# Attention and a dense block on one core: all products as 64x32 weights in two row halves of TensorE

## The chip, the core and the metric

The kernel runs on one core of a Trainium2 chip. A core has TensorE (PE; its weight loads are shown apart as PEld), VectorE (DVE), ScalarE (ACT), GpSimd (POOL) and SyncE (SP), which work side by side and wait for each other on semaphores. Each engine runs its own list of instructions in order. Products land in PSUM, which has 8 banks of 128 partitions x 512 fp32 values; ScalarE and VectorE read them from there. The metric is the time of one execution in device microseconds; lower is better.

## What is computed

One layer on 2,048 rows of 640 values: a layer norm, and then the sum of the input, an attention block and a dense block, both on the normalised rows.

```python
B, S, D, H = 1, 2048, 640, 32;  Dh = D // H          # 20 values a head
q = (xn @ wq).reshape(B, S, H, Dh).transpose(0, 2, 1, 3)
k = xn @ wk                                          # one key and one value head
v = xn @ wv                                          # for all 32 query heads
p = softmax(einsum("bhqd,bkd->bhqk", q, k) * Dh ** -0.5)
o = einsum("bhqk,bkd->bhqd", p, v)
A = o.transpose(0, 2, 1, 3).reshape(B, S, H * Dh) @ wo
h = relu(xn @ w1 + b1) ** 2                          # 1,536 wide
out = x + A + (h @ w2 + b2)
```

## The kernel before

**Scores and exponentials.** The work is cut into 32 blocks (`NBLK`): 4 chunks of 512 queries by 8 groups of 4 heads. A block has 16 key tiles of 128 keys, and each key tile with a head is one score tile of 128 keys x 512 queries in one PSUM bank, 2,048 score tiles in all. A score tile is one matmul: the 20 rows of a head lie at partitions 32h to 32h+19 of `qT`, and of `kT`, which holds the keys four times, once for each head's place. So the weights are 20x128 at row position 32h (tile size 32x128), and up to four heads run at once in the four row groups, into different banks.

A score tile takes one of two ways. On the first, ScalarE does the exponential of two neighbouring banks (sometimes three or one) in one instruction (L1056) into `PT`. On the second, a *set* of one key tile and its four heads: VectorE writes the bits of a piecewise linear power of two from PSUM (L1245), GpSimd (L1265) or VectorE (L1267) makes three copies shifted by a constant, and a DMA with an add, issued by GpSimd (L1280), or VectorE may sum pairs of them. A set then enters the value product with up to four terms, the last two with scaled values `vxs`.

**Value products.** The values with a column of ones are the weights (`vx`, 128 keys x 32 columns, tile size 128x32), and the four heads go to the four column strips of one bank at once: four matmuls, one group. All products of a block add up in bank 7 (`PVB`), block after block; `emit_norm` copies the sum out (L1124), inverts the row of sums and brings both to the output layout by DMA.

**Dense work.** Queries, the first dense layer (L767, L775 behind it), the second dense layer with the output projection: all are `Unit`s, lists of chunks of four matmuls on the four column strips (`col4`, L561; `mm`, L426, is the line that all these matmuls have in the profile). One unit is open at a time, in a bank of its own. A 512-wide chunk is one fifth of a product over 640 rows; the 320-wide chunks are half a row of the output. The last row chunk's dense part is made early and parked in DRAM. The residual is loaded in 32 halves, and VectorE adds the bias to each (L823) before the output's evacuation adds it to the product (L854, L839).

**What sets the order.** No order is written out. While the program is built, a planner inside the kernel keeps a time for every engine, has a duration for every operation and takes, again and again, the operation that can start first, with priorities by kind. `make_step` picks the banks for ScalarE's next step, `make_dqk` opens a set, `make_pv` and `make_dpv` the value products, `pool_banks` says which banks may be taken by others. Its parameters change every 10 us of planned time (`RULES`). What comes out is one fixed list for each engine. TensorE's changes between the tile sizes 32x128 and 128x32 are charged in it (`SWITCH`), and matmuls that find no work ready may be filled with products of zeros (`fill_parts`).

Of the kernel before, what the change touches and what calls it, by code (L numbers as in the profile page):

```python
# [7 lines left out]
BF16 = mybir.dt.bfloat16  # L8
# [4 lines left out]
ALU = mybir.AluOpType  # L13
# [25 lines left out]
def _pl(z):  # L39
# [9 lines left out]
NB = 7  # L49
# [26 lines left out]
XSP = 1.0  # L76
# [6 lines left out]
SWITCH = 0.105  # L83
ACB, ACM = 0.0631, 0.4267
# [5 lines left out]
            fr=[f"OUT{16 + k // 2}.16" for k in range(8)])  # L90
# [8 lines left out]
RULES = {1: {'DGAP': 1.5, 'DLAST': 3.5, 'EPS': 0, 'M1T': 0.9, 'ADP': 0.35, 'R3': 2, 'D1P': 0.5, 'ND': 1, 'KEEP': 1, 'ADPM': 0.9, 'KEEPM': 3, 'DVL': 1.8},  # L99
         2: {'EVP': 1.1, 'DGAP': 0.5, 'IDLE': 0.3, 'EPS': 0.06, 'M1': 0, 'M1T': 0.9, 'ADP': 5, 'R3': 9, 'PP': 4, 'ND': 2, 'KEEP': 0, 'ADPM': 0.9, 'KEEPM': 3, 'PVA': 1},  # L100
         3: {'EVP': 1.1, 'DGAP': 0.5, 'IDLE': 0.3, 'EPS': 0.12, 'M1': 0, 'M1T': 2, 'ADP': 5, 'R3': 9, 'PP': 4, 'ND': 2, 'KEEP': 0, 'ADPM': 0.9, 'KEEPM': 3, 'JIT': 0.8},
         4: {'DGAP': 1.5, 'DLAST': 3.5, 'EPS': 0, 'M1T': 0.9, 'ADP': 0.9, 'R3': 2, 'D1P': 0.5, 'ND': 2, 'KEEP': 1, 'KEEPM': 1, 'DVL': 1.8, 'ADDB': 1, 'KEEPX': -1},
         5: {'DGAP': 1.5, 'DLAST': 3.5, 'EPS': 0, 'M1T': 0.9, 'ADP': 0.9, 'R3': 2, 'D1P': 0.5, 'ND': 2, 'KEEP': 1, 'ADPM': 0.9, 'KEEPM': 3, 'DVL': 1.8},
         6: {'DGAP': 1.5, 'DLAST': 3.5, 'EPS': 0, 'M1T': 0.9, 'ADP': 0.9, 'R3': 2, 'D1P': 0.5, 'ND': 2, 'KEEP': 1, 'ADPM': 0.9, 'KEEPM': 3, 'DVL': 1.8, 'SQP': 2},
         7: {'DGAP': 1.5, 'DLAST': 3.5, 'EPS': 0, 'M1T': 0.9, 'ADP': 0.9, 'R3': 2, 'D1P': 0.5, 'ND': 2, 'KEEP': 1, 'KEEPM': -1, 'DVL': 1.8, 'DQP': 0.5},
         8: {'DGAP': 1.5, 'DLAST': 3.5, 'EPS': 0, 'M1T': 0.9, 'ADP': 0.9, 'R3': 2, 'D1P': 0.5, 'ND': 2, 'KEEP': 1, 'DVL': 1.8, 'DQP': 0.5},
         9: {'DGAP': 1.5, 'DLAST': 3.5, 'EPS': 0, 'M1T': 0.9, 'ADP': 0.9, 'R3': 2, 'D1P': 0.5, 'ND': 2, 'KEEP': 1, 'ADPM': 0.9, 'KEEPM': 3, 'DVL': 1.8},
         11: {'DGAP': 1.5, 'DLAST': 3.5, 'EPS': 0, 'M1T': 0.9, 'ADP': 0.9, 'R3': 2, 'D1P': 0.5, 'ND': 2, 'KEEP': 1, 'KEEPM': 1, 'DVL': 1.8},
         12: {'DGAP': 1.5, 'DLAST': 3.5, 'EPS': 0, 'M1T': 0.9, 'ADP': 0.9, 'R3': 2, 'D1P': 0.5, 'ND': 2, 'KEEP': 1, 'KEEPM': 1, 'DVL': 1.8},
         13: {'ADP': 0.9, 'PBIAS': -1},  # L110
         14: {'DGAP': 1.5, 'DLAST': 3.5, 'EPS': 0, 'M1T': 0.9, 'ADP': 0.35, 'R3': 2, 'D1P': 0.5, 'ND': 2, 'KEEP': 1, 'KEEPM': 1, 'DVL': 1.8},
         15: {'DGAP': 1.5, 'DLAST': 3.5, 'EPS': 0, 'M1T': 0.9, 'ADP': 0.35, 'R3': 2, 'D1P': 0.5, 'ND': 2, 'KEEP': 1, 'KEEPM': 1, 'DVL': 1.8, 'ADPM': 3.5},
         16: {'EVP': 1.1, 'DGAP': 0.5, 'IDLE': 0.3, 'EPS': 0.06, 'M1': 0, 'M1T': 0.9, 'ADP': 5, 'R3': 9, 'PP': 4, 'ND': 2, 'KEEP': 0, 'ADPM': 0.9, 'KEEPM': 3},
         17: {'EVP': 1.1, 'DGAP': 0.5, 'IDLE': 0.3, 'EPS': 0.06, 'M1': 0, 'M1T': 0.9, 'ADP': 5, 'R3': 9, 'PP': 4, 'ND': 2, 'ADPM': 0.9, 'KEEPM': 3, 'KEEPX': 2},
         18: {'EVP': 1.1, 'DGAP': 0.5, 'IDLE': 0.15, 'EPS': 0.06, 'M1': 0, 'M1T': 0.9, 'ADP': 5, 'R3': 9, 'PP': 4, 'ND': 2, 'KEEPM': 3, 'KEEPX': 2, 'NOPEN': 3},
         19: {'EVP': 1.1, 'DGAP': 0.5, 'IDLE': 0.15, 'EPS': 0.06, 'M1': 0, 'M1T': 0.9, 'ADP': 5, 'R3': 9, 'PP': 4, 'ND': 2, 'KEEPM': 3, 'KEEPX': 2, 'NOPEN': 3},
         20: {'EVP': 1.1, 'DGAP': 0.5, 'IDLE': 0.15, 'EPS': 0.06, 'M1': 0, 'M1T': 0.9, 'ADP': 5, 'R3': 9, 'PP': 4, 'ND': 2, 'KEEPM': 3, 'KEEPX': 3, 'NOPEN': 3, 'BEHIND': 0.3},
         21: {'DGAP': 1.5, 'EPS': 0, 'M1T': 0.9, 'ADP': 0.9, 'R3': 2, 'D1P': 0.5, 'ND': 2, 'KEEP': 1, 'KEEPM': 0, 'DVL': 0.6},
         22: {'P2': 2, 'M1T': 2, 'KEEPM': 0, 'ADDM': 1.5},
         23: {'DLAST': 3.5, 'ADDB': 1},  # L120
         24: {'DGAP': 1.5, 'DLAST': 3.5, 'EPS': 0, 'M1T': 0.9, 'ADP': 0.9, 'R3': 2, 'D1P': 0.5, 'ND': 2, 'KEEP': 1, 'ADPM': 0.9, 'KEEPM': 3, 'DVL': 1.8},
         25: {'DGAP': 1.5, 'DLAST': 3.5, 'EPS': 0, 'M1T': 0.9, 'ADP': 0.9, 'D1P': 0.5, 'ND': 2, 'KEEP': 1, 'ADPM': 0.9, 'KEEPM': 3, 'DVL': 1.8},
         26: {'DGAP': 0},
         27: {'DGAP': 0, 'URG': 6, 'PVA': 1.05},
         28: {'DGAP': 1.5, 'DLAST': 3.5, 'EPS': 0, 'M1T': 0.9, 'ADP': 0.9, 'R3': 2, 'D1P': 0.5, 'ND': 2, 'KEEP': 1, 'ADPM': 0.9, 'KEEPM': 3, 'DVL': 1.8},
         29: {'DGAP': 0, 'DLAST': 3.5, 'EPS': 0, 'M1T': 0.9, 'ADP': 0.9, 'R3': 1, 'D1P': 0.5, 'ND': 2, 'KEEP': 1, 'ADPM': 0.9, 'KEEPM': 3, 'DVL': 1.8, 'KEEPX': -1},
         30: {'DGAP': 0, 'DRATE': 0.7, 'IDLE': 0.15, 'URG': 4, 'M1': 2, 'M1T': 2, 'ADP': 3.5, 'R3': 9, 'KEEPM': 0, 'KEEPX': 1, 'ADDM': 1.5},
         31: {'DGAP': 1.5, 'DLAST': 3.5, 'EPS': 0, 'M1T': 0.9, 'ADP': 0.9, 'R3': 2, 'D1P': 0.5, 'ND': 2, 'KEEP': 1, 'KEEPM': 1, 'DVL': 1.8, 'MRG': 0, 'MPRIO': 0.3},
         32: {'DGAP': 1.5, 'DLAST': 3.5, 'EPS': 0, 'M1T': 0.9, 'ADP': 0.9, 'R3': 2, 'D1P': 0.5, 'ND': 2, 'KEEP': 1, 'KEEPM': 1, 'DVL': 99, 'KEEPX': -1},
         33: {'DGAP': 1.5, 'DLAST': 3.5, 'EPS': 0, 'M1T': 0.9, 'ADP': 0.9, 'D1P': 0.5, 'ND': 2, 'KEEP': 1, 'KEEPM': 1, 'DVL': 1.8, 'P2': 1, 'PVD': 0.9},  # L130
         34: {'DGAP': 1.5, 'DLAST': 3.5, 'EPS': 0, 'M1T': 0.9, 'ADP': 0.9, 'R3': 2, 'D1P': 0.5, 'ND': 2, 'KEEP': 1, 'KEEPM': 1, 'DVL': 1.8},
         35: {'EVP': 1.1, 'DGAP': 0.5, 'IDLE': 0.3, 'EPS': 0.06, 'M1': 0, 'M1T': 0.9, 'ADP': 5, 'R3': 9, 'PP': 4, 'ND': 2, 'KEEP': 0, 'ADPM': 0.9, 'KEEPM': 3, 'P2': 1},
         36: {'EVP': 1.1, 'DGAP': 0.5, 'IDLE': 0.3, 'EPS': 0.06, 'M1': 0, 'M1T': 0.9, 'ADP': 5, 'R3': 9, 'PP': 4, 'ND': 2, 'KEEP': 0, 'ADPM': 0.9, 'KEEPM': 3},
         37: {'EVP': 1.1, 'DGAP': 0.5, 'IDLE': 0.3, 'EPS': 0.06, 'M1': 0, 'M1T': 0.9, 'ADP': 5, 'R3': 9, 'PP': 4, 'ND': 2, 'KEEP': 0, 'ADPM': 0.9, 'KEEPM': 3},
         38: {'EVP': 1.1, 'DGAP': 0.5, 'IDLE': 0.3, 'EPS': 0.06, 'M1': 0, 'M1T': 0.9, 'ADP': 5, 'R3': 9, 'PP': 4, 'ND': 2, 'KEEP': 0, 'ADPM': 3.5, 'KEEPM': 3},
         39: {'EVP': 1.1, 'DGAP': 0.5, 'IDLE': 0.3, 'EPS': 0.06, 'M1': 0, 'M1T': 0.9, 'ADP': 5, 'R3': 9, 'PP': 4, 'ND': 2, 'KEEP': 0, 'ADPM': 3.5, 'KEEPM': 3},
         41: {'DGAP': 1.5, 'DLAST': 3.5, 'EPS': 0.06, 'M1T': 0.9, 'ADP': 0.9, 'R3': 9, 'D1P': 0.5, 'ND': 2, 'KEEP': 1, 'KEEPM': 1, 'DVL': 1.8},
         42: {'DGAP': 1.5, 'DLAST': 3.5, 'EPS': 0.06, 'M1T': 0, 'ADP': 0.9, 'R3': 9, 'D1P': 0.5, 'ND': 2, 'KEEP': 1, 'KEEPM': 1, 'DVL': 1.8, 'BEHIND': 0.3},
         43: {'DGAP': 1.5, 'DLAST': 3.5, 'EPS': 0.06, 'M1T': 0, 'ADP': 0.9, 'R3': 9, 'D1P': 0.5, 'ND': 2, 'KEEP': 1, 'KEEPM': 1, 'DVL': 1.8, 'BEHIND': 0.3, 'URG': 6},
         44: {'EVP': 1.1, 'DGAP': 0.5, 'IDLE': 0.3, 'EPS': 0.06, 'M1': 0, 'M1T': 0.9, 'ADP': 5, 'R3': 9, 'PP': 4, 'ND': 2, 'KEEP': 0, 'ADPM': 0.9, 'KEEPM': 3},  # L140
         45: {'DGAP': 0, 'DRATE': 0.7, 'IDLE': 0.15, 'URG': 4, 'M1': 2, 'M1T': 2, 'ADP': 3.5, 'R3': 9, 'KEEPM': 0, 'KEEPX': 1, 'PP': 4, 'PVD': 1},
         46: {'EVP': 1.1, 'DGAP': 0.5, 'IDLE': 0.3, 'EPS': 0.06, 'M1': 0, 'M1T': 0.9, 'ADP': 5, 'PP': 4, 'ND': 2, 'KEEP': 0, 'ADPM': 0.9, 'KEEPM': 3, 'DQP': 0.5},
         47: {'DGAP': 1.5, 'DLAST': 3.5, 'EPS': 0, 'ADP': 0.9, 'R3': 2, 'D1P': 0.5, 'ND': 2, 'KEEP': 1, 'ADPM': 0.9, 'KEEPM': 3, 'DVL': 1.8, 'DQP': 0.5, 'P2': 2},
         48: {'EVP': 1.1, 'DGAP': 0.5, 'IDLE': 0.3, 'EPS': 0.06, 'M1': 0, 'M1T': 0.9, 'ADP': 5, 'R3': 9, 'PP': 4, 'ND': 2, 'KEEP': 0, 'ADPM': 0.9, 'KEEPM': 3},
         50: {'DGAP': 1.5, 'DLAST': 3.5, 'EPS': 0, 'M1T': 0.9, 'ADP': 0.9, 'R3': 2, 'D1P': 0.5, 'ND': 2, 'KEEP': 1, 'KEEPM': 1, 'DVL': 1.8, 'M1': 2},
# [88 lines left out]
class Op:  # L234
    def __init__(self, name, eng, dur, parts, deps=(), lat=None, lock=False, mode="C", prio=3, dma=None):
# [14 lines left out]
        if dma is not None:  # L250
            dma.n += 16
            self.tgt = (dma, dma.n)
# [1441 lines left out]
```

## Time and profile before

| | us |
|---|---|
| median of 3 runs | 676.48 |
| lowest, highest | 676.47, 681.13 |
| span of the profiled execution | 688.3 |
| busy in it: PE, ACT, DVE, POOL | 679.9, 657.7, 607.2, 586.2 |

The page of the profile gives each engine's busy time and, in 40 equal slices of the span, its share in tenths; a line of the same kind gives the clock that TensorE was granted. Other views group instructions by line and shape (busy time, mean length of one, idle time ahead of them), list who waited for whom, give busy time in chosen stretches, and list instructions in order of time. A matmul's length is modelled: about 0.39 us for 512 columns, though groups follow each other more closely, so that distances between starts tell more than lengths.

### The profile page before, as it was taken

The page shows a single profiled execution, that of the slowest core. Times are in us where ns is not written, and L with a number is a line of the kernel's source. Part 1 is how long each engine was busy: PE and PEld are TensorE (multiplying, and loading weights), DVE is VectorE, ACT ScalarE, POOL GpSimd, SP SyncE. Part 2 cuts the span into 40 slices and gives each one's busy share as a digit, 9 for nine tenths or more (in the row PEclk, how much of TensorE's full clock was granted, in tenths as well). Part 3 has the DMA queues.
Part 4 walks back from the last instruction along what each step waited for, and adds up shares of the span by engine and source line. Part 5 has one row for each costly group of instructions (what it writes and reads, how often), then busy time and mean ns, then how long its engine had stood idle before and what let it go on. Part 6 is the DMA issues. An engine that isn't in the chain of part 4 may idle for free.

```text
span 688.3 us, 22356 instructions
## 1 busy us (share of the span) xinstructions
PE 679.9 (99%) x9554; PEld 212.3 (31%) x9555; DVE 607.2 (88%) x1081; ACT 657.7 (96%) x721; POOL 586.2 (85%) x597
## 2 busy tenths in 40 slices
PE   8999999999999999999999999999999999999998
PEld 4233222232322222333332222333332222233334
DVE  8558999899999899889998999889888999999893
ACT  6668999999999999999999999999999999999994
POOL 0406989889999999989999989999989998989982
PEclk9559999999999999999999999999999999999999
DMA  8355677767877697768977667677777765788873
GB/s 215 89 130 145 130 158 149 152 138 156 168 166 143 124 176 136 155 133 179 200 140 154 134 131 136 135 150 147 141 160 152 141 124 115 152 180 185 169 158 97
DMA packets 62894, 102.21 MB, mean 148 GB/s; under 512 B 22418, under 2 KB 40722, under 8 KB 62794
## 3 DMA queue, kind: packets, MB, share of 16 engines
q0 software_dynamic: 19296, 70.26, 54.8%
q1 hardware_dynamic: 41898, 30.14, 16.6%
q8 instruction: 75, 1.23, 0.7%
q10 hardware_dynamic: 1600, 0.38, 0.3%
q14 instruction: 25, 0.20, 0.1%
HBM read 17.71 MB, written 4.42 MB: 32 GB/s over the span
## 4 chain that ended last, share of the span: by engine, by line
PE 74%; ACT 15%; POOL 5%; DVE 3%; DMA 2%; issue 1%; DVEq 0%; POOLq 0%
PE ps L426 71%; ACT PT L1056 15%; POOL x_sb L1265 2%; DVE tmore L1245 2%; POOL tmore L1265 2%; PE ps L619 1%; DMA x_sb<-x_sb 1%; DMA tmore<-tmore 1%; PE ps L648 1%; POOL x_sb L1280 1%; DVE big L775 0%; DVE xr L823 0%; DVE out_sb L1346 0%; PE ps L581 0%; PE ps L576 0%
## 5 line engine op out<-in xcount | busy, mean ns | idle before, releaser
L1056 ACT ACTIVATE PT<-ps 128x1024 bf16<-128x1024 f32 (+2 forms) x697 | 644.7, 1107 | 16.1 <-PE ps L426 15.5
L1245 DVE TENSOR_SCALAR tmore<-ps 128x512 uint16<-128x512 f32 x644 | 417.9, 682 | 43.9 <-PE ps L426 37.9
L1265 POOL INT64_ADD tmore<-tmore x226 | 258.8, 1306 | 35.9 <-DVE tmore L1245 25.9
L426 PE MATMUL ps<-qT,kT 20*128 20x512 bf16 x2048 | 277.1, 390 | 1.2 <-ACT PT L1056 0.8
L1265 POOL INT64_ADD x_sb<-tmore x222 | 255.8, 1287 | 21.4 <-PE ps L426 4.7
L426 PEld LDWEIGHTS ps<-qT,kT 20*128 20x128 bf16 x2048 | 68.8, 91 | 265.0 <-ACT PT L1056 218.4
L426 PE MATMUL ps<-PT,vx 128*32 128x512 bf16 x1396 | 139.5, 395 | 0.1
L426 PE MATMUL ps<-xnT,w_sb 128*32 128x512 bf16 x960 | 79.3, 383 | 0.4 <-DVE tmore L1245 0.4
L426 PE MATMUL ps<-w_sb,big 128*32 128x320 bf16 x1536 | 79.2, 301 | 0.3
L1280 POOL DMA_DIRECT2D tmore<-tmore x65 | 71.2, 1112 | 2.5 <-POOL tmore L1265 2.4
L1280 POOL DMA_DIRECT2D x_sb<-tmore x65 | 67.7, 1048 | 4.8 <-POOL x_sb L1265 3.3
L426 PE MATMUL ps<-tmore,vxs 128*32 128x512 bf16 x640 | 58.3, 382 | 0.3 <-POOL tmore L1265 0.3
L426 PE MATMUL ps<-x_sb,vxs 128*32 128x512 bf16 x624 | 57.6, 383 | 0.2 <-DMA x_sb<-x_sb 0.2
L426 PEld LDWEIGHTS ps<-PT,vx 128*32 128x32 bf16 x1396 | 35.2, 93 | 73.1 <-issue 67.5
L426 PE MATMUL ps<-tmore,vx 128*32 128x512 bf16 x456 | 43.3, 382 | 0.4 <-DMA tmore<-tmore 0.4
L426 PEld LDWEIGHTS ps<-w_sb,big 128*32 128x32 bf16 x1536 | 34.3, 96 | 28.4 <-issue 16.8
L767 DVE TENSOR_SCALAR hT_tmp<-ps,b1col 128x512 bf16<-128x512 f32 x48 | 35.5, 740 | 0.9 <-PE ps L426 0.6
L426 PE MATMUL ps<-xnT,wq_sb 128*32 128x512 bf16 (+2 forms) x480 | 35.8, 366 | 0.2 <-ACT PT L1056 0.2
L426 PE MATMUL ps<-wo_c,OC 128*32 128x320 bf16 x608 | 31.6, 301 | 0.0
L426 PE MATMUL ps<-x_sb,vx 128*32 128x512 bf16 x320 | 31.3, 382 | 0.0
L775 DVE TENSOR_TENSOR big<-hT_tmp 128x512 bf16<-128x512 bf16 x48 | 28.2, 589 | 0.2
L426 PEld LDWEIGHTS ps<-xnT,w_sb 128*32 128x32 bf16 x960 | 19.8, 95 | 22.0 <-issue 15.4
(103 smaller groups left out, 324.5 us busy)
## 6 DMA issues: line engine op xcount, KB each, us to landing
x_sb<-tmore POOLq DMA_DIRECT2D x65, 512.0 KB, 5.4
tmore<-tmore POOLq DMA_DIRECT2D x65, 512.0 KB, 5.6
w_sb<-in_B_w_dram SPq DMA_DIRECT2D x8, 480.0 KB, 4.3
big<-OR SPq DMA_DIRECT2D x71, 40.0 KB
big<-drs SPq DMA_DIRECT2D x71, 40.0 KB
xh<-in_A_x_dram SPq DMA_DIRECT2D x32, 80.0 KB, 3.4
out_dram<-out_sb SPq DMA_DIRECT2D x15, 160.0 KB, 2.8
qT<-QCr SPq DMA_DIRECT2D x105, 20.0 KB
```

The lines of the kernel that those rows point to most:

```text
L426: return lambda e: e.matmul(out_, l, r, start=start, stop=stop, tile_position=tp)
L619: return [lambda e: e.matmul(ps[:, PVB, :], ones_bf[:, :], hT_tmp[:, 0, :], start=True, stop=True)]
L648: return [(lambda e, dt=dt: e.transpose(out=psbf(bk)[:, dt * 128:(dt + 1) * 128], in_=xn_sb[:, st, dt * 128:(dt + 1) * 128], identity=iden ...
L767: o = Op(f"RL{qc}_{f}", "DVE", 0.66, [lambda e: e.tensor_scalar(out=hT_tmp[:, k % 2, :], in0=ps[:, bk, :], scalar1=b1col[:, f:f + 1], scal ...
L775: q = op(f"SQ{qc}_{f}", "DVE", 0.34, lambda e: e.tensor_tensor(out=h2T[:, f, :], in0=hT_tmp[:, k % 2, :], in1=hT_tmp[:, k % 2, :], op=ALU. ...
L1056: return Op(f"ACT{st_['j']}", "ACT", ACB + ACM * n, [lambda e: e.activation(out=to, in_=ps[:, b0:b0 + (n - 1) * db + 1:db, :], func=AF.Exp ...
L1245: d1 = op(f"D1_{n}_{i}", "DVE", 0.60, lambda e: e.tensor_scalar(out=L[:, cs].bitcast(U16), in0=ps[:, bank, :], scalar1=XA, scalar2=XB, op0 ...
L1265: fn = lambda e, T=T, j=j: e.int64_add(out=T.bitcast(I64), in0=L.bitcast(I64), in1=TSTEP * j * 0x0001000100010001)
L1280: p = op(f"AD{a}_{n}", "POOL", ADDUR, lambda e, src=src, dst=dst: e.dma_start(dst, src, accum_op=ALU.add), dp + [ad_last.get(k)], dma=adse ...
```

## The change

Behind the opening, every product has weights of 64 rows x 32 columns (tile size 64x32), so that the array is two row halves of four column strips. Each half is a *lane* with groups of four matmuls of its own.

- A 128-row product becomes two half groups, one in each lane, that add into the same bank. The lanes need not do their halves at the same time. A change of lane on a bank waits on a semaphore until the other lane's last group is done (`lane_ctr`; waits of TensorE for itself did not exist before).
- A score tile becomes one half group: the 64 rows hold two heads' places, and the four column strips take 32 keys each. `kT` is kept twice: copy 0 has the places of heads 0 and 2, copy 1 those of heads 1 and 3, the others multiplied by zero (`kmask`), so that one head of the pair is picked. Key and query weights are padded to 32 columns, and `qT` is set to zero once where no query is written. VectorE makes the second copy.
- All eight banks are in one pool; a block's sum may lie in any bank, and two blocks' sums may be open at once. ScalarE's step takes any two neighbouring banks, or three where many are free.
- Two (in one stage three) dense units may be open at once.
- The bias is no longer added to the residual by VectorE: an identity weight adds it on TensorE as the first chunk of each output half, and the evacuation takes the residual as loaded.
- The planner has a time for each lane, other constants, and new `RULES`. Merging of score groups of different kinds into one visit (`MRG`, `M1`, `P2`) is gone.

```diff
-NB = 7
+NB = 8
+SLOT, SLOT3, XLANE = 0.216, 0.136, 0.255
+HORD = (0, 2, 1, 3)
...
-        kT = sb("kT", [128, S], BF16)
+        kT = sb("kT", [128, 2, S], BF16)
...
         def start_of(op, r, switch=True):
+            if op.eng == "PE":
+                if op.lane is not None:
+                    s = max(r, pe_last[0], lanes[op.lane])
+                    if pe_mode[0] != "S":
+                        s = max(s, max(lanes) + (SWITCH if switch else 0.0))
+                    return s
...
+        def lane4(lane, lhs, rhs, bank, n, first, last):
+            w = slice(64 * lane, 64 * lane + 64)
+            return [mm(ps[32 * j:32 * j + 32, bank, 0:n], lhs(j)[w], rhs[w], first, last, (64 * lane, 32 * j)) for j in range(4)]
+
+        def key_parts(cs, src, k):
+            return lambda e: e.tensor_scalar(out=kT[:, k, cs], in0=src, scalar1=nk0[:, 1:2], scalar2=kmask[:, k:k + 1], op0=ALU.add, op1=ALU.mult)
...
+        def bias_chunk(cs):
+            return [(SLOT3, lambda lane, first, last: lane4(lane, lambda j: ident[:, 0:32], b2bc[:, cs], ub[0], 320, first, last))]
...
-            xs_op[n] = op(f"XS{n}", "DVE", 0.40, lambda e: e.tensor_tensor(out=xr[:, k % NXR, :], in0=xh[:, k % NXR, :], in1=b2bc[:, cs], op=ALU.add), [xr_op[n], l_b2, old], lock=True, prio=XSP)
...
-                parts.append(mm(ps[:, banks[k], :], kT[32 * h:32 * h + DH, kt * 128:(kt + 1) * 128], qT[32 * h:32 * h + DH, b % NQS, :], True, True, (32 * h, 0)))
-            qk = Op(f"QK{j}", "PE", 0.215, parts, deps, mode="R")
...
+        def qk_parts(b, kt, h, bank):
+            return lane4(h // 2, lambda j: kT[:, h % 2, kt * 128 + 32 * j:kt * 128 + 32 * j + 32], qT[:, b % NQS, :], bank, 512, True, True)
...
+        def pv_op(name, b, lane, wgt, srcs, deps, last, new_bank):
+            p = pvb.get(b)
+            if p is None:
+                deps.append(bank_rel[new_bank])
+            elif lane != p["lane"]:
+                deps.append(p["op"])
+            bank = new_bank if p is None else p["bank"]
+            w = slice(64 * lane, 64 * lane + 64)
+            parts = [mm(ps[32 * h:32 * h + 32, bank, :], wgt[w], srcs[h][w], p is None, last, (64 * lane, 32 * h)) for h in range(HPG)]
+            return Op(name, "PE", SLOT, parts, deps, lane=lane)
...
-                elif k == len(o.parts) - 1 and o.consumed:
-                    v = add(lists[o.eng], fn, waits=w, inc=eng_ctr[o.eng])
+                elif k == len(o.parts) - 1 and o.consumed:
+                    c = eng_ctr[o.eng] if o.lane is None else lane_ctr[o.lane]
+                    v = add(lists[o.eng], fn, waits=w, inc=c)
```

698 lines of the change are left out of this document (343 added, 355 removed), and 8 rows, old and new, of the table RULES.

## The prediction

> **What bounds the kernel now.** I read the page's busy shares and slices first, then ScalarE by stretches, then the groups, the waits and the raw order of TensorE in one short window.
>
> ```profile
> span 688.3 us, 22356 instructions
> PE 679.9 (99%) x9554; PEld 212.3 (31%) x9555; DVE 607.2 (88%) x1081; ACT 657.7 (96%) x721; POOL 586.2 (85%) x597
> ACT  6668999999999999999999999999999999999994
> PEclk9559999999999999999999999999999999999999
> 14.00:60.00 46.00, 44.94 (x471) 14.32 (x470) 28.01 (x81) 30.89 (x31) 11.65 (x14) 0.59 0.53 129
> 60.00:660.00 600.00, 597.39 (x8420) 180.04 (x8418) 551.84 (x921) 598.45 (x653) 559.79 (x565) 1.00 0.75 149
> 680.00:689.00 9.00, 4.93 (x140) 3.38 (x132) 5.56 (x12) 0.00 (x0) 0.00 (x0) 1.00 0.21 75
> ACT PT L1056 <- PE ps L426: 15.5, 23, 1.7
> ...
> 13.99 1.02 ACT L1056 ACTIVATE PT<-ps 128x1024 bf16<-128x1024 f32 x1 [0.81 <-PE ps L426]
> 268.08 14.81 ACT L1056 ACTIVATE PT<-ps 128x1024 bf16<-128x1024 f32 x16
> 674.72 4.68 ACT L1056 ACTIVATE PT<-ps 128x1536 bf16<-128x1536 f32 x4
> ```
>
> The rows by stretches give busy time and count of PE, PEld, DVE, ACT, POOL, then the clock. From 60 to 660 us ScalarE is busy for 598.45 of 600 us and TensorE for 597.39: both are full at once. ScalarE's waits for TensorE are 15.5 us in all, and the 14 to 60 us stretch, where it is busy for only 30.89 of 46, holds nearly all of them. There the granted clock is 0.59 on average and 0.5 in two slices; after that it is 1.00. The last three rows (start, length) are ScalarE's first exponentials, an undisturbed run of 16, and the last ones, which end at 679.4.
>
> **The base of the sum.** The profiled execution spans 688.3 us, the median of the runs is 676.48: 11.8 us less. I put this on the half clock, since the stretch that has it is the only one in which ScalarE starves (15.1 of its 46 us) and 11.8 fits inside. So the sum is made on the span and 11.8 us is taken off: a timed run is 14.0 us before the first exponential, ScalarE's stretch of 679.4 - 14.0 - 11.8 = 653.6, and 688.3 - 679.4 = 8.9 us behind it: 676.5.
>
> **Part 1: ScalarE's work.** The order of the built programs has 671 exponentials of two tiles, 14 of three and 12 of one before (and 4 of two into other buffers), 1,404 tiles; after, 696 of two, one of three and one of one, 1,396 tiles.
>
> ```profile
> L1056 ACT ACTIVATE PT<-ps 128x1024 bf16<-128x1024 f32 x671 | 623.4, 1107 | 14.3 <-PE ps L426 13.8
> L1056 ACT ACTIVATE PT<-ps 128x1536 bf16<-128x1536 f32 x14 | 20.3, 1502 | 1.7 <-PE ps L426 1.7
> L1056 ACT ACTIVATE PT<-ps 128x512 bf16<-128x512 f32 x12 | 8.0, 663 | 0.0
> ```
>
> A tile more costs (1502 - 663)/2 = 420 ns. Eight tiles fewer are 8 x 0.42 = **-3.4 us**, on the path, as ScalarE is full. "Any neighbouring banks" does not make steps larger: the triples go from 14 to 1. This work bounds the gain. The undisturbed run takes (14.81 - 1.107)/15 = 0.914 us a step of two; by it the work before is 675 x 0.914 + 14 x 1.334 + 12 x 0.494 = 642 us of the 653.6, and after 696 x 0.914 + 1.334 + 0.494 = 638. So before loses 12 us in all to waits and short delays, and no better feeding can bring more than that.
>
> **Part 2: TensorE's work.** The rows of one window (start, length, matmuls) give the price of a score group between the other products.
>
> ```profile
> 299.71 0.39 PE L426 MATMUL ps<-qT,kT 20*128 20x512 bf16 x4
> 300.03 0.40 PE L426 MATMUL ps<-PT,vx 128*32 128x512 bf16 x4
> 300.26 0.72 PE L426 MATMUL ps<-w_sb,big 128*32 128x320 bf16 x16
> 300.91 0.39 PE L426 MATMUL ps<-qT,kT 20*128 20x512 bf16 x2
> 301.23 0.32 PE L426 MATMUL ps<-w_sb,big 128*32 128x320 bf16 x4
> ...
> 664.44 0.39 PE L426 MATMUL ps<-x_sb,vx 128*32 128x512 bf16 x4
> 664.65 0.39 PE L426 MATMUL ps<-x_sb,vxs 128*32 128x512 bf16 x4
> ```
>
> Groups of four 512-wide products start 664.65 - 664.44 = 0.21 us apart (I take 0.215; 300.26 - 300.03 gives 0.23). Four 320-wide groups last 0.72 against 0.32 for one: (0.72 - 0.32)/3 = 0.135 each. A score group holds the engine 301.23 - 300.91 = 0.32 us, so 0.32 - 0.215 = 0.10 is the change of tile size; ahead of it the same again, 300.91 - 300.26 - 4 x 0.135 = 0.11. The order has 685 visits to score groups, 1,215 groups of 512 and 552 of 320: 685 x 0.42 + 1215 x 0.215 + 552 x 0.135 = 288 + 261 + 75 = 624 us.
>
> After, the 1,379 changes of tile size fall to 29. A 2,048-tile score pass becomes 2,048 half-array groups of four. In all the order has 4,516 half groups of 512, 1,136 of 320 (the bias rows that replace the VectorE add among them: 32 of these, 32 x 0.135/2 = 2 us) and 60 of 256 at about 0.11: (4516 x 0.215 + 1136 x 0.135 + 60 x 0.11)/2 = 565 us with both halves always full. They are not: TensorE runs its list in order, and in 1,065 places a group follows one on its own half, so the other half stays empty behind it. Walking the order with these durations, a group starting neither before the one ahead of it nor before its half is free, gives 618 us.
>
> New too are 616 waits of TensorE for itself: products of both halves add into one bank, so a change of half on a bank waits until the other half's last product has landed. 356 of the 616 stand at a value product of ScalarE's tiles. Behind each stand, in the same list, the next score groups, for which ScalarE waits. The trace of before has no such wait. The nearest row is ScalarE waiting for a score group:
>
> ```profile
> 303.85 0.39 PE L426 MATMUL ps<-qT,kT 20*128 20x512 bf16 x2
> 304.28 1.02 ACT L1056 ACTIVATE PT<-ps 128x1024 bf16<-128x1024 f32 x1 [0.19 <-PE ps L426]
> ```
>
> From start to the waiter's start are 304.28 - 303.85 = 0.43 us. Walking the order again with 0.43 from the awaited group's start gives 632 us; with no wait beyond the slot 621; with the 0.10 of a tile-size change on top (0.53) 654. I take 632, the row that also ends in a semaphore wait for a product. Most are covered: 429 of the 616 have two or more groups of the waiter's own half between. So TensorE needs 621 to 654, likely 632, against 624: **+8 us of work (-3 to +30), no relief**. It has that room: the window from its first score group to its end is about 660 us without the slow clock. I price it at 0 to +2 us of time, with 0 taken as long as the need stays under some 645 us; beyond that every microsecond counts.
>
> [...] Before has 9,554 matmuls, the new order 23,167. In the trace the four matmuls of a group start within 10 ns (0.40 us for x4, where one lasts 395 ns by its group's row below). [...]
>
> **Part 3: VectorE, GpSimd, banks.**
>
> ```profile
> L426 PE MATMUL ps<-PT,vx 128*32 128x512 bf16 x1396 | 139.5, 395 | 0.1
> L1245 DVE TENSOR_SCALAR tmore<-ps 128x512 uint16<-128x512 f32 x644 | 417.9, 682 | 43.9 <-PE ps L426 37.9
> L823 DVE TENSOR_TENSOR xr<-xh,b2bc 128x320 f32<-128x320 bf16 x32 | 22.2, 696 | 0.0
> L1267 DVE TENSOR_SCALAR x_sb<-tmore 128x2048 uint16<-128x2048 uint16 x18 | 14.0, 775 | 0.1
> L663 DVE TENSOR_SCALAR kT<-ps,nk 128x256 bf16<-128x256 f32 x6 | 2.9, 484 | 11.0 <-PE ps L426 10.9
> L1265 POOL INT64_ADD tmore<-tmore x226 | 258.8, 1306 | 35.9 <-DVE tmore L1245 25.9
> L1280 POOL DMA_DIRECT2D tmore<-tmore x65 | 71.2, 1112 | 2.5 <-POOL tmore L1265 2.4
> ```
>
> VectorE loses 32 bias adds (-22.2). It gains 18 shifted copies (53 against 35, 18 x 0.775 = +14.0), 8 score tiles (8 x 0.682 = +5.5) and the second key copy (6 x 0.484 + 4 x 0.35, its row in part 4, = +4.3): +1.6 in all, and it is idle for 48 us between 60 and 660. GpSimd loses 12 copies and 12 sum DMAs, 12 x 1.306 + 12 x 1.112 = -29. SP issues the same 596 instructions. All this is cover, not path: 0. Eight banks in one pool with the value sums wandering among them (450 of 1,756 half groups in bank 7, the rest in others) free no engine that is late.
>
> **Part 4: opening and end.** The second key copy stands ahead of the first scores.
>
> ```profile
> 12.06 1.12 ACT L602 ACTIVATE qT<-ps 128x128 bf16<-128x128 f32 x4 [0.34 <-PE ps L426]
> 12.30 0.35 DVE L600 TENSOR_SCALAR kT<-ps,nk 128x128 bf16<-128x128 f32 x1
> ```
>
> The query copies on ScalarE end at 12.06 + 1.12 = 13.18; two key copies of 0.35 us from 12.30 end at 13.0. So the copies hide the second one: 0, or +0.35 if they were gone. At the end the sum of the last block and the last output halves each need a change of half, 0.43 - 0.215 = 0.2 each: +0.4.
>
> Sum: 676.5 - 3.4 + 0.4 + (0 to 2) = 673.5 to 675.5, less what falls of the 12 us that ScalarE loses, now that any two neighbouring banks serve it and a score group needs no change of tile size: between 0 and 12, and I take 3, a quarter, as TensorE is as full as before. That is **671 us**, -0.8%.
>
> **The rivals.** One per cent (6.8 us) is what a measurement of this kernel tells from no change.
>
> - *The plan hides every change of half.* TensorE needs 621 us, ScalarE runs at its undisturbed rate: 14.0 + 638 + 8.9 = 661 us. For it: 429 of 616 are well covered. Against it: it means that all 12 us go, the opening's too.
> - *The changes of half cost more (the other side).* Place: the value products, 356 of the waits, with scores queued behind. Price: 0.53 us from the awaited start, a need of 654, 22 more than taken: 671 + 22 = 693 us. It decides from a need of about 645. For it: the list is strict, and the need climbs by 22 us for 0.10 us of wait.
> - *The clock stays at a half in the opening of the timed runs:* 671 + 11.8 = 683 us. The profiled run of before had it, two of three timed runs seem not to. [...]
> - *Matmul starts have a floor.* The widest bound from rows is 0.135/4 = 34 ns per matmul, as 320-wide strips never went faster: 22,848 x 0.034 = 777 us, so 671 + 777 - 632 = 816 us.
> - *The change doesn't do what it says:* the halves don't run beside each other. Then 2 x 565 = 1,130 us of slots, and some 1,160 us. Before shows four column strips at once and up to four row groups at once, never both.
>
> **How the numbers follow.** Chances: forecast 0.45 (its own range 666 to 678), hidden 0.22, dearer changes 0.17, slow clock 0.08, start floor 0.05, halves in turn 0.03. Faster by over 1% (under 669.7): 0.22 and three tenths of the forecast, 0.36. Slower (over 683.2): 0.17 + 0.04 + 0.05 + 0.03 = 0.29. Within: 0.35. The range 660 to 692 leaves out the last two, a third of the dearer case and a tail of the fastest: under 0.2.
>
> **What would show it.** Part 1: 698 exponentials of about 1.1 us, and ScalarE busy for 598 of 600 us again. Part 2: half groups of both halves 0.21 us apart on each half, no 0.10 at scores, waits of TensorE for itself that end 0.43 us behind the awaited start. If ScalarE idles on TensorE between 60 and 660 us, I am wrong by Part 2; if the eight starts of a pair spread over 0.2 us, the floor holds. Half clock outside the opening would be wrong for all cases.

## The result and the profile after

The changed kernel takes **815.86 us** (median of its runs) against 676.48: ratio 1.205, 95% interval 1.197 to 1.212. It is slower by a fifth; the forecast was 671, its range ended at 692. The profiled execution has a span of 813.7 us. One of the three executions fell into a slower state (830.04 us), and runs that were made only once (experiments 2, 3, 5, 6 and 8 to 10) can't be told apart in this way, so that steps of some 2% between them mean little.

The page of the profile after: span, busy time by engine, ScalarE's busy tenths, the granted clock, the queue that brings instructions, and the chain that ended last.

```profile
span 813.7 us, 50344 instructions
...
PE 724.5 (89%) x23167; PEld 413.6 (51%) x23167; DVE 611.4 (75%) x1089; ACT 669.3 (82%) x718; POOL 560.6 (69%) x574
...
ACT  7859889877888787788798988897999989997760
...
PEclk9979999999999899999999999999999999999999
...
q8 instruction: 181, 2.97, 1.5%
...
PE 83%; issue 10%; POOL 3%; DVE 3%; DMA 1%; ACT 0%; DVEq 0%; POOLq 0%
```

ScalarE no longer stands at 9 in every slice, and no slice shows half clock. "Issue" is 10% of the chain: time in which an engine waited for nothing that the profile shows. The window between opening and end, with the columns of the prediction's window (busy time and count of PE, PEld, DVE, ACT, POOL, then clock, DMA share and GB/s):

```profile
60.00:780.00 720.00, 642.07 (x20921) 365.28 (x20913) 555.67 (x921) 620.09 (x657) 539.39 (x546) 0.98 0.60 120
```

The list of waits of the same run (us in total, times, longest):

```profile
PEld ps L443 <- issue: 126.9, 161, 3.4
...
ACT PT L1105 <- PE ps L443: 113.0, 105, 3.6
PE ps L443 <- issue: 76.5, 73, 3.1
...
PEld ps L443 <- PE ps L443: 33.2, 104, 1.1
```

Everyone now waits for TensorE: ScalarE is busy for 620 of 720 us, where it was 598 of 600. TensorE waits for "issue" first; its waits for itself, the changes of half, come far behind. Of the two rows of "issue", that of the matmuls (PE) is the one to go by. The weight loads had even more of it in the kernel before, but in short waits that the matmuls covered; the matmuls themselves waited 0.9 us for it there, in two places.

```profile
PEld ps L426 <- issue: 175.6, 705, 0.8
```

One such place in order of time (start, length, and in brackets the idle time ahead with what ended it):

```profile
295.63 3.98 ACT L1105 ACTIVATE PT<-ps 128x1024 bf16<-128x1024 f32 x4
302.84 2.89 ACT L1105 ACTIVATE PT<-ps 128x1024 bf16<-128x1024 f32 x3 [3.23 <-PE ps L443]
...
302.28 0.61 PE L443 MATMUL ps<-qT,kT 64*32 64x512 bf16 x11 [3.13 <-issue]
```

TensorE stands still for 3.13 us with nothing to wait for, and ScalarE for 3.23 us right behind it.

Split by ScalarE's exponentials: in the kernel before, 14.0 us lie ahead of the first, 653.6 us (half clock taken off) between first and last, 8.9 behind. After, it is 14.8, 774.4 and 24.5: +0.8, +120.8 and +15.6. Of the 120.8, ScalarE's idle time between exponentials is 109 (114.0 against 16.7 less the 11.8 of half clock). Most of the other 12 goes with the pauses too: exponentials in a row start 0.905 us apart (the median in the kernel before), though one behind a pause lasts 1.02. A pause so loses an overlap of 0.115 us, and 82 pauses more (105 against 23) lose 9.4. The base of the prediction is a little off here: a run's time is 1.8 us more than its span (815.51 against 813.7), so that not 11.8 but 13.6 us had to come off the span before. With that the three parts add up to the 139 us between the two times.

**Where TensorE stands still.** An instruction packet on queue 8 is 16,384 bytes and there is one for every 256 of TensorE's matmuls and weight loads: 46,334/181 after. The kernel before had this row, which I had not read:

```profile
q8 instruction: 75, 1.23, 0.7%
```

It had 19,109 of them: 255 a packet. I took all gaps of over 0.35 us between starts on TensorE and set them beside the packets' transfers. After has 164 such gaps, 145.0 us in all; 104 of them, 117.0 us, end 1.1 to 1.75 us behind the end of a packet's transfer, and their places in the list step by 255.6 instructions a packet. Before, 4 gaps (2.2 us) do, no more than chance would put there: the 0.65 us behind each of 75 packets are 7% of the span, and it has 94 gaps. After, chance alone would give some 24 of the 164, but 93 of the 104 (112 us) also lie within 12 instructions of one even grid. From the start of a packet's transfer to the first instruction behind such a gap it is 2.1 to 3.3 us, median 2.42.

### The profile page after: what moved, and what is told of

The parts are those of the page before. It is cut to its first block, busy times and chain, and to the rows that moved or that the text cites. A ratio compares the mean times of both kernels' runs of the same rounds, so it can differ in the third digit from the quotient of the medians.

```text
span 813.7 us, 50344 instructions
## 1 busy us (share of the span) xinstructions
PE 724.5 (89%) x23167; PEld 413.6 (51%) x23167; DVE 611.4 (75%) x1089; ACT 669.3 (82%) x718; POOL 560.6 (69%) x574
## 4 chain that ended last, share of the span: by engine, by line
PE 83%; issue 10%; POOL 3%; DVE 3%; DMA 1%; ACT 0%; DVEq 0%; POOLq 0%
PE ps L443 82%; DVE tmore L1359 1%; POOL tmore L1379 1%; PE ps L649 1%; POOL x_sb L1379 1%; DMA xnT<-big 1%; POOL tmore L1394 0%; POOL x_sb L1394 0%; DVE OR L1224 0%; PE ps L705 0%; ACT PT L1105 0%; PE ps L609 0%; PE ps L604 0%; PE ps L737 0%; DVE big L517 0%
## 5 line engine op out<-in xcount | busy, mean ns | idle before, releaser
L1105 ACT ACTIVATE PT<-ps 128x1024 bf16<-128x1024 f32 (+1 forms) x694 | 656.6, 1034 | 114.8 <-PE ps L443 113.0
L443 PE MATMUL ps<-qT,kT 64*32 64x512 bf16 x8192 | 510.0, 385 | 27.6 <-issue 25.7
L1359 DVE TENSOR_SCALAR tmore<-ps 128x512 uint16<-128x512 f32 x652 | 423.0, 685 | 118.5 <-PE ps L443 114.8
L443 PE MATMUL ps<-PT,vx 64*32 64x512 bf16 x2776 | 273.8, 385 | 7.5 <-issue 5.4
L443 PEld LDWEIGHTS ps<-qT,kT 64*32 64x32 bf16 x8192 | 163.0, 91 | 150.5 <-issue 42.8
L443 PE MATMUL ps<-w_sb,big 64*32 64x320 bf16 x3072 | 150.7, 303 | 16.3 <-issue 16.2
L443 PE MATMUL ps<-xnT,w_sb 64*32 64x512 bf16 x1920 | 141.0, 382 | 6.0 <-issue 6.0
L443 PE MATMUL ps<-x_sb,vxs 64*32 64x512 bf16 x1296 | 124.1, 385 | 5.4 <-issue 5.0
L443 PE MATMUL ps<-tmore,vxs 64*32 64x512 bf16 x1272 | 119.0, 381 | 6.6 <-issue 5.0
L443 PE MATMUL ps<-tmore,vx 64*32 64x512 bf16 x1016 | 100.1, 383 | 0.3 <-POOL tmore L1379 0.2
L443 PEld LDWEIGHTS ps<-w_sb,big 64*32 64x32 bf16 x3072 | 78.7, 94 | 38.3 <-issue 22.1
```

The source lines that it names most:

```text
L443: return lambda e: e.matmul(out_, l, r, start=start, stop=stop, tile_position=tp)
L1105: return Op(f"ACT{st_['j']}", "ACT", ACB + ACM * n, [lambda e: e.activation(out=to, in_=ps[:, b0:b0 + (n - 1) * db + 1:db, :], func=AF.Exp ...
L1359: d1 = op(f"D1_{n}_{i}", "DVE", 0.60, lambda e: e.tensor_scalar(out=L[:, cs].bitcast(U16), in0=ps[:, bank, :], scalar1=XA, scalar2=XB, op0 ...
```

## The experiments

Three theories, by the letters that the expectations use. **D**: TensorE's list is delivered in packets of 256 instructions, too slowly for 23,167 matmuls with a weight load each. **H**: the waits between the row halves cost more than the 0.43 us that the prediction took. **M**: each matmul start has a price of its own (34 ns, the prediction's fourth rival). One table for all runs of a whole kernel; "gaps" are those at packets, counted as above, and the idle time is that of ScalarE ahead of its pairs of score tiles.

| run | matmuls + loads | packets | gaps, us | ScalarE idle, us | time, us |
|---|---|---|---|---|---|
| kernel before | 19,109 | 75 | 4, 2.2 | 14.3 | 676.5 |
| kernel after | 46,334 | 181 | 104, 117.0 | 114.8 | 815.9 |
| one strip | 22,598 | 88 | 2, 1.1 | 22.7 | 702.0 |
| one strip, more loads | 34,466 | 135 | 28, 26.2 | 32.8 | 716.4 |
| one strip in scores | 34,046 | 133 | 34, 37.7 | 39.5 | 727.8 |
| one strip in dense work | 36,638 | 143 | 32, 29.9 | 40.1 | 725.1 |
| plan spaced by 0.108 us | 46,006 | 180 | 81, 102.8 | 120.6 | 833.1 |
| plan spaced by 0.145 us | 45,326 | 177 | 66, 38.0 | 55.6 | 898.3 |
| kernel before, more loads | 26,157 | 102 | 4, 2.1 | 4.5 | 683.6 |
| fewer, larger matmuls | 23,402 | 92 | 1, 0.5 | 414.3 | 1,167.4 |

**1. The same plan with fewer instructions.**

```diff
-return [mm(ps[32 * j:32 * j + 32, bank, 0:n], lhs(j)[w], rhs[w], first, last, (64 * lane, 32 * j)) for j in range(4)]
+return [mm(ps[32 * j:32 * j + 32, bank, 0:n], lhs(j)[w], rhs[w], first, last, (64 * lane, 32 * j)) for j in range(STRIPS)]
```

`STRIPS` is 1. In experiments 1 to 4 the first warm-up products of the opening also go to all eight banks instead of one.

> The changed kernel with the same planned order, the same waits, the same banks and the same exponentials, but every half group of a score tile, of a dense step and of an output product sends only the first of its four 64x32 matmuls (columns 0 to 31); the value products keep all four. Three quarters of the scores and of the dense sums are so not computed. TensorE's list falls from 23,167 matmuls to 11,299, the instruction packets from 181 to about 90. Theory D (delivery of instructions: TensorE gets its list in packets of 256 instructions, and a packet takes 2.1 to 3.3 us from its start to the first instruction out of it, some 3.5 us from packet to packet, so that more than 256 instructions in 3.5 us run dry): the starts no longer wait at packets, ScalarE's exponentials stand beside one another again, and the time falls to 665 to 690 us, about where the recorded sum put it. Theory H (the waits between the two row halves cost more than 0.43 us): all 616 waits are still there, the time stays over 780. Theory M (a start price for each matmul, 34 ns): 11,299 times 34 ns is 384 us, so it would fall as well, but no gap would stand at the packets in the changed kernel's trace, where 104 do.

Measured: 702.0 us, ratio 1.036 (1.033 to 1.040). Its page and waits:

```profile
q8 instruction: 88, 1.44, 0.8%
...
L1110 ACT ACTIVATE PT<-ps 128x1024 bf16<-128x1024 f32 (+1 forms) x694 | 642.8, 1063 | 22.7 <-PE ps L444 21.6
```

```profile
PEld ps L444 <- PE ps L444: 28.9, 96, 0.6
...
ACT PT L1110 <- PE ps L444: 21.6, 24, 6.0
...
PEld ps L444 <- issue: 10.5, 43, 0.6
```

Of the 139 us between the two times, 114 are gone, and with them the waits for "issue": the loads' row falls from 126.9 us to 10.5, none longer than 0.6, and the matmuls' row of 76.5 us is empty. Three quarters of the products of scores and dense work are gone as well; experiment 4 takes that up. TensorE's waits for itself are nearly all still there (28.9 against 33.2), so theory H, which asked for over 780, falls as the main cause. But the expectation was missed too: 702 lies 12 us above its upper end. Even with its list at hand this plan is 25 us behind the kernel before. By the same split: +0.5 ahead of the first exponential, +14.8 in the stretch, +9.8 behind the last (18.7 us). In the stretch ScalarE idles 21.8 us, 7.0 of them from 20 to 60 us and 8.1 behind 660. Pieces of the chain there (start, length, what):

```profile
651.77 6.67 DMA drs<-R
...
660.57 7.06 DMA big<-drs
...
668.79 29.65 PE ps L444 x328
```

The last sums' way through DRAM and back, and behind it 29.65 us of TensorE with outputs and the last products, set the end.

**2 and 3. One strip in the scores alone, and in the dense work alone.** The scores in `qk_parts`, then the dense layer's and the output's calls of `lane4`.

```diff
-    return lane4(h // 2, lambda j: kT[:, h % 2, kt * 128 + 32 * j:kt * 128 + 32 * j + 32], qT[:, b % NQS, :], bank, 512, True, True)
+    return lane4(h // 2, lambda j: kT[:, h % 2, kt * 128 + 32 * j:kt * 128 + 32 * j + 32], qT[:, b % NQS, :], bank, 512, True, True)[:1]
```

> The changed kernel with only the first of the four 64x32 matmuls of each half group of the scores; dense steps, output and value products whole. Three quarters of the scores are not computed. 17,023 matmuls, about 134 instruction packets in place of 181. Theory D: at 3.5 us from packet to packet the floor is 134 times 3.5 = 469 us in place of 634 us, with bursts in the dense steps still running dry: 690 to 740 us, and the gaps at packets fall from 104 to 30 to 60. Theory H: over 780 us.

> The changed kernel with only the first of the four 64x32 matmuls of each half group of the dense layer (both weights) and of the output products; scores, queries, keys and values whole. Three quarters of those dense sums are not computed. 18,319 matmuls, about 144 instruction packets in place of 181, but the stretches with scores and value products stay as thick with instructions as in the changed kernel. Theory D, between the two runs on record (17,023 matmuls: 727.8 us, 11,299: 702.0) and the changed kernel (23,167: 815.9): 725 to 760 us, gaps at packets between 30 and 80. Theory H: over 780.

Measured: 727.8 and 725.1 us, both as theory D had it, the second at the very edge of its range. The count of gaps (34 and 32) is at the low end of what was expected. Whichever part of the list is thinned, about as many instructions give about the same time.

**4. The instructions without the work.** Experiments 1 to 3 leave out products as well as instructions. Here instructions that do nothing are put back.

```diff
+PADS = 3
...
+def padded(e):
+    for _ in range(PADS):
+        e.ldweights(zeros32[w], tile_position=(64 * lane, 0))
+    return e.matmul(ps[0:32, bank, 0:n], lhs(0)[w], rhs[w], start=first, stop=last, tile_position=(64 * lane, 0))
+return [padded]
```

> The run with the first of four matmuls only (702.0 us, ratio 1.036), same matmuls, plan, waits and banks, and ahead of each matmul that stands for a half group three weight loads of zeros that nothing uses: 11,868 more instructions and no more products. Three quarters of the scores and of the dense sums are not computed. About 134 instruction packets in place of 88, as many as the run with the scores cut (133; 727.8 us). Four loads of 23 ns each (three extra loads a matmul took 92 ns a matmul when measured alone) fit under a half group of 215 ns. Theory D, the count of instructions alone: gaps at packets come back, 20 to 60, and the time goes up to 715 to 740 us. If instead the matmuls left out were what the shorter runs saved: 700 to 706 us, no gaps.

Measured: 716.4 us, ratio 1.060 (1.055 to 1.064), against 1.036 (1.033 to 1.040) without the loads.

```profile
q8 instruction: 135, 2.21, 1.2%
...
L1114 ACT ACTIVATE PT<-ps 128x1024 bf16<-128x1024 f32 (+1 forms) x694 | 649.2, 1034 | 32.8 <-PE ps L592 26.5
```

The gaps at packets come back, 28 with 26.2 us, and the time rises by 14 us, though no product was added. It is less than the 26 us of experiment 2 at the same count. The loads stand in other places, and that run was taken once only; what makes the difference was not tried.

**5. The delivery by itself.**

```diff
+def both(form, n, count):
+    for g in range(count):
+        form(0, (2 * g) % 8, n)
+        form(1, (2 * g + 1) % 8, n)
+    mark()
...
+both(half, 512, 200)
+both(half, 320, 200)
+both(half, 128, 200)
```

`half` is four 64x32 matmuls in one row half, as in `lane4`; `mark` is twelve full-array products that set the stretches apart.

> TensorE alone, on zeros; nothing of the reference is computed and the output is zeros. One after the other: 200 times both row halves (eight 64x32 matmuls) at 512 columns, at 320, at 128; 200 groups of one half at 512; 200 pairs of 64x128 matmuls at 512 and 320 and 400 pairs at 128; then 60 half groups of 512 columns that change halves each time behind a semaphore. Theory D, at 3.5 us for a packet of 256 instructions or 27 ns for a matmul with its weight load: 27 to 28 ns a matmul with both halves at 512 (the work alone asks 26.9), 27 at 320 (the work: 16.7) and 27 at 128 (the work: 6.7), with gaps every 256 instructions; 54 ns with one half alone; the 64x128 pairs are bound by work at 512 and 320 (0.215 and 0.136 us a pair). Theory M, a start price of 34 ns: 34 ns a matmul in all three stretches with both halves, evenly spread. Theory H: a half that waits for the other starts more than 0.5 us behind it; the recorded sum had 0.43.

Measured, per matmul from the first start of a stretch to the last: 28.0 ns at 512 columns, 26.8 at 320, 27.3 at 128; one half alone at 512 53.8; pairs of 64x128 at 512 0.215 us. The stretch at 320 columns in order of time, then that at 128:

```profile
65.02 3.86 PE L308 MATMUL ps<-mv,wt 64*32 64x320 bf16 x215
69.87 2.37 PE L308 MATMUL ps<-mv,wt 64*32 64x320 bf16 x128 [0.99 <-issue]
73.33 2.37 PE L308 MATMUL ps<-mv,wt 64*32 64x320 bf16 x128 [1.09 <-issue]
77.05 2.37 PE L308 MATMUL ps<-mv,wt 64*32 64x320 bf16 x128 [1.36 <-issue]
...
117.24 1.91 PE L308 MATMUL ps<-mv,wt 64*32 64x128 bf16 x128 [2.46 <-issue]
120.97 1.91 PE L308 MATMUL ps<-mv,wt 64*32 64x128 bf16 x128 [1.82 <-issue]
124.70 1.91 PE L308 MATMUL ps<-mv,wt 64*32 64x128 bf16 x128 [1.82 <-issue]
```

This is theory D by itself: exactly 128 matmuls, which with their loads are 256 instructions, then a hole, and 3.45 to 4.01 us from one such run to the next, however short the matmuls are. The windows of the three stretches (length, PE busy, PEld busy, ..., clock):

```profile
17.20:62.10 44.90, 44.44 (x1601) 25.10 (x1600) 0.00 (x0) 0.00 (x0) 1.00 0.02 4
65.00:108.00 43.00, 29.49 (x1601) 25.11 (x1600) 0.00 (x0) 0.00 (x0) 1.00 0.02 5
110.70:154.50 43.80, 22.55 (x1601) 20.01 (x1600) 0.00 (x0) 0.00 (x0) 0.56 0.02 4
```

Three stretches with 1,600 matmuls take 43 to 45 us each, though PE is busy for 44, 29 and 23 of them; even half clock (0.56) in the third changes nothing. The DMA share is 0.02, so the delivery is slow without any other traffic. From the start of a packet's transfer to the first matmul behind a hole it is 2.48 us (median), as in the changed kernel (2.42). Between the holes the matmuls start 16.4 ns apart on average at 320 columns and 11.8 at 128, and the first eight of each stretch, four in each half, start within 24 ns: theory M's 34 ns, evenly spread, falls.

**6. Half changes, changes of tile size and loads by themselves.** One half group of 512 columns waits for the other half's, eight in a row; then 64x32 and 64x128 in turn; then a half with more loads.

```diff
+e.wait_ge(hop[1 - k], n[1 - k])
+half(k, g, 512)[3].then_inc(hop[k], 1)
...
+half(0, 0, 512); half(0, 2, 512)
+wide(0, 4, 512); wide(0, 6, 512)
...
+e.ldweights(wt[0:64, 0:32], tile_position=(0, 0))
```

> TensorE alone, on zeros; nothing of the reference is computed and the output is zeros. 20 sets of 24 full-array matmuls and 8 half groups of 512 columns that change halves behind a semaphore; 100 times both halves as 64x32 at 512 columns and then both as 64x128; the same in one half alone; one half with 1 and with 3 more weight loads for each matmul; 2,560 weight loads alone. Half changes at full clock: theory H asks over 0.5 us from start to start, the recorded sum 0.43. A change between 64x32 and 64x128, from the run with 2,613 of them: 0.2 to 0.25 us each beyond the work. Weight loads: theory D asks 13.7 ns for each instruction where the list is thick, so 13.7 ns or more for a load alone, and gaps every 256; at 3 more loads the group takes 20 instructions, 0.274 us or more in place of 0.215.

Measured: a half that waits for the other starts 0.460 us behind the last matmul that it waits for (133 of 140 at 459 to 461 ns; the other seven, 494 to 676, stand in stretches that run into half clock), and 0.47 behind that group's first. The prediction's 0.43 from the group's start was short by 0.04, not by the 0.10 of its second rival. Of the changes of tile size, inside one half (start, length):

```profile
292.86 0.61 PE L308 MATMUL ps<-mv,wt 64*32 64x512 bf16 x8
293.40 0.60 PE L312 MATMUL ps<-mv,wt 64*128 64x512 bf16 x2
293.93 0.61 PE L308 MATMUL ps<-mv,wt 64*32 64x512 bf16 x8
```

Two groups of 0.215 us and a change take 293.40 - 292.86 = 0.54 us, so the change is 0.11; the 0.2 to 0.25 us that were expected are wrong. With both halves changing together, the halves still start 3 ns apart and one size follows the other in 0.32 us. One extra load a matmul leaves 53.8 ns a matmul. Three make it 60 at full clock, with holes at three places 51 matmuls apart, which with four loads each are 255 instructions; behind 468 us the clock is at half, and it is 106. The 92 ns that the expectation of experiment 4 uses is an average over both.

**7. More instructions in the kernel before.** Its 128x32 weight loads are sent twice.

```diff
+PADS = 1
...
+for _ in range(PADS if tuple(l.shape) == (128, 32) else 0):
+    e.ldweights(l, tile_position=tp)
+return e.matmul(out_, l, r, start=start, stop=stop, tile_position=tp)
```

> The kernel before, whole, with each of its 7,048 weight loads of 128x32 sent twice: 26,157 instructions on TensorE in place of 19,109, about 102 packets in place of 75. One extra load a matmul was free when measured alone (53.8 ns a matmul with and without). Theory D: its thick stretches come to 12 instructions for each 0.215 us, 56 per us, about what a packet begun with 135 instructions still to go can keep up with (135 in 2.42 us), so a few gaps appear, 5 to 30 in place of 4, and the time stays or grows a little: 676 to 695 us.

Measured: 683.6 us, ratio 1.011 (1.009 to 1.014). The time is in the expected range, but the gaps at packets stay at 4, where 5 to 30 were expected, so the 8 us are not shown to come from delivery. At 102 packets a list as even as this one was still delivered in time.

**8 and 9. A plan that knows of the delivery.** `pe_last` is the planner's time of the last start on TensorE.

```diff
-s = max(r, pe_last[0], lanes[op.lane])
+s = max(r, pe_last[0] + 0.108, lanes[op.lane])
```

The second run has 0.145 in the same place.

> The changed kernel, whole, its plan made again with one more rule: the start of a half group stands at least 0.108 us behind the start of the one ahead of it (four matmuls at 27 ns). Matmuls 23,003, so as many packets, and the same layout; only the order and what is put beside what differ. Theory D: the chip delivered no more than that anyway, so nothing is lost by it, and the order is now one that the delivery can keep: by the planner's own reckoning its list ends 46 us later than that of the changed kernel, and if the chip keeps it, the time falls from 816 to 735 to 770 us, still above the kernel before. If the loss came from something that the order does not know (half changes, starts), the time stays at 800 to 830 or grows by the 46 us to 860.

> The changed kernel, whole, with the plan's least distance between starts of half groups at 0.145 us in place of 0.108 (36 ns a matmul in place of 27). The planner's own list then ends 136 us later than the one made with 0.108. The run with 0.108 missed: 833 us, its gaps at packets still 103 us in 81. Theory D with what the traces show of a packet's start (begun when about 135 instructions are still to go, usable 2.42 us later): 0.108 asks for 135 instructions in 1.8 us and runs dry each time, 0.145 asks for them in 2.45 us and just does not. So the gaps at packets should all but go (under 25 of some 177), and the chip should keep this plan: 865 to 900 us in all, 136 us more of plan less about 90 us of gaps. If delivery only kept an average (3.5 us a packet) the plan with 0.108 should have gone through, so gaps that stay as they were at 0.145 (over 60) speak against this form of the theory; the time would be 940 to 970.

Measured: 833.1 us with 0.108, a clear miss, in the very range (800 to 860) that was to speak for a loss of another kind; and 898.3 with 0.145. What tells the two apart is how the chip keeps the plan, read at the end of the last exponential. The plan of the changed kernel has it at 664.0 us, the chip at 789.2: 125 us late. With 0.108: 708.9 and 811.5, 103 late. With 0.145: 765.3 and 770.0, **5 late**, over the whole list (3 to 5 from 60 us on). So here one half group in 0.145 us, 36 ns a matmul, was kept and one in 0.108 was not. All three plans price the changes of half alike, so these are not what made two of them late. In the changed kernel, by the grid of its gaps, a packet's transfer began when a median of 135 instructions ahead of it were still to start. At 13.5 ns each they last 1.8 us, less than the 2.42 that the packet needs; at 18 ns, 2.45. That is an estimate from medians: for half of the packets the count lies between 94 and 163. Why a list at 27 ns a matmul, the average of experiment 5, falls behind in the kernel was not tried. The matmuls' waits for "issue" with 0.108, then with 0.145:

```profile
PE ps L443 <- issue: 70.7, 61, 3.1
...
PE ps L443 <- issue: 7.6, 12, 1.2
```

Not all of the expectation came true: 66 gaps at packets are counted, where under 25 were expected and over 60 were to speak against it. But this trace has 412 gaps of over 0.35 us from all causes, and the 0.65 us behind each of 177 packets are 13% of the span, so that some 53 would fall there by chance: the count says little here. They are short, 38.0 us in all (0.58 us each against 1.13 in the changed kernel), and the 940 to 970 us that were to go with them did not come. The 898 us lie in the expected range partly by luck: behind the last exponential the plan has 99 us, and the chip took 126, most of it at half clock.

**10. The same products in fewer, larger matmuls.** The whole layout with half the instructions: four strips as one 64x128 matmul where the weights lie beside one another.

```diff
+def lane1(lane, lhs, rhs, bank, n, first, last):
+    w = slice(64 * lane, 64 * lane + 64)
+    return [mm(ps[:, bank, 0:n], lhs[w], rhs[w], first, last, (64 * lane, 0))]
```

> The changed kernel, whole, but with the four 64x32 matmuls of a half group written as one 64x128 matmul wherever their weights lie beside one another (scores, most dense steps, output products); value products stay 64x32. 11,701 matmuls in place of 23,167, and 2,613 changes of tile size in place of 29. Theory D: packets fall to about 92, no gaps at them; but each change of size costs the 0.10 us of the kernel before and keeps the halves from overlapping over it, so 565 + 261 = 826 us of TensorE at least, 820 to 900 us in all. If changes between 64x32 and 64x128 cost nothing: 670 us.

Measured: 1,167.4 us, far above the expected 820 to 900.

```profile
PE 1159.0 (99%) x11701; PEld 354.1 (30%) x11701; DVE 634.9 (54%) x1089; ACT 719.7 (62%) x718; POOL 559.9 (48%) x574
...
q8 instruction: 92, 1.51, 0.5%
```

One gap at a packet is left, as theory D has it, and TensorE is the bound all the same. The 2,613 changes at 0.11 are 287 us, 852 with the slots' 565. The rest goes with halves that stand alone, as the trace shows. At 2,595 of the 2,605 changes behind the opening the first matmul of the new size starts over 0.2 us behind the last of the old one, 0.31 at 512 columns and 0.23 at 320, together 789 us. So at these a group didn't run beside one of the other size. And of the 2,606 stretches between changes 1,373 hold one half group only, with the other half of the array empty.

No run beats the kernel before.

## Why the prediction was wrong, point by point

- **The step that failed is Part 2, TensorE's work.** It priced each group by what its columns take and each change of half by its wait, and took for granted that the list of instructions is always at hand. The change raises the count of matmuls with their loads from 19,109 to 46,334, and no term of the sum was for that. In the changed kernel's trace, gaps of 117 us stand at the packets; 114 of the 139 us go when the list is halved, with part of the products gone too (experiment 1); instructions that do nothing bring 14 us back (4); and the delivery is as slow alone (5). To ask whether the need stays under 645 us was the right question, with a need from the wrong resource: 181 packets, of which about 100 left TensorE waiting.
- **The changes of half.** 0.43 us from the awaited group's start was taken, 0.47 measured. By the prediction's own slope (22 us for 0.10) the need becomes 632 + 9 = 641 us, still under 645. This size was a little off; the rival with 0.53 and 693 us is not what happened.
- **The rival with a start floor** gave 816 us, and the time came out at 816, but not by its mechanism: within a packet matmuls start 11.8 to 16.4 ns apart, and the first eight of both halves within 24 ns, where it asked for over 0.2 us. That the two numbers agree is luck. It had the right thing to count, matmuls, and a wrong place for the price.
- **Part 1, ScalarE's work.** The stretch less its idle time is 648.8 us before (665.4 - 16.7) and 646.5 in the run with one strip (668.4 - 21.8): -2.3, where -3.4 was forecast. This holds. Of the 12 us that ScalarE was said to lose before, 2 are the slip in the base.
- **No relief, and 3 of ScalarE's 12 us won back.** Wrong by itself: with the list at hand ScalarE idles 21.8 us, where the kernel before has 3 to 5 without its half clock. The halves' waits for each other, the opening and the sums' way through DRAM may all have a part in it; they were not tried apart, so the cause of the 25 us by which that run is behind the kernel before stays open.
- **Part 4, the end.** +0.4 us was forecast; it was +15.6, and +9.8 with the list at hand. The prediction counted two changes of half there and not what this plan leaves behind the last exponential.
- **Halves beside each other, and the clock.** The halves do run beside each other (eight starts in 24 ns), and no half clock of any weight shows (no slice under 0.7 in the changed kernel); these rivals were rightly small. VectorE and GpSimd never set the pace, as Part 3 had it.

## What to carry to other kernels

Count the instructions, not only the columns: a split into smaller matmuls at full array use multiplies what must be delivered (here from 19,109 to 46,334), and the queue of instruction packets on the page gives packets over span (75 in 688.3 us before, 181 in 813.7 after). Here a list of 19,109 or 26,157 matmuls and loads in 680 us hardly waited, and one of 46,334 lost over 110 us. To tell a slow delivery from a slow engine, look for waits of the matmuls for "issue" that come every 256 instructions right behind a packet's transfer (here every 255.6, ending 1.1 to 1.75 us behind it).

## What the runs showed of the hardware that was not expected

- TensorE ran dry at the edge of a packet: at 320 and 128 columns in experiment 5, 128 matmuls with their loads, then 1 to 2.5 us of nothing, 3.45 to 4.01 us from one such run to the next, with next to no other DMA traffic (0.02). In the changed kernel, too, a packet holds 256 instructions (46,334/181). From its medians, 135 instructions still to start when a transfer begins and 2.42 us until the packet is of use, an estimate is that the delivery falls behind there where the list is thicker than some 56 instructions per us.
- In the kernel the delivery kept up with less than alone: 27 ns a matmul on the average alone, but in the kernel 0.108 us a half group (27 ns a matmul) could not be kept and 0.145 could. The packets' way took as long in both (2.42 and 2.48 us).
- In experiment 10 groups of different tile sizes did not run beside each other: at 2,595 of 2,605 changes the new size starts over 0.2 us behind the old one.
- In experiment 5 the first eight 64x32 matmuls, in both row halves, start within 24 ns, and 200 such groups at 512 columns take 44.8 us: at that width the work (26.9 ns a matmul, half of the 53.8 of one half alone) and the delivery (26.8 and 27.3 at 320 and 128 columns) just balance, and at 320 and 128 columns the groups took nearly as long (43 and 43.8 us).
